# The first transfers and the first gates of a gated linear attention kernel, put in another order

## The chip, the cores and the metric

The kernel runs on one core of one Trainium2 chip. Its engines work side by side, each through its own instructions in program order: PE (TensorE) multiplies matrices, DVE (VectorE) and POOL (GpSimd) work element by element, ACT (ScalarE) computes functions such as Exp and Ln, and SP (SyncE) issues most of the transfers (DMAs) from the main memory. Semaphores make one engine wait for another or for a transfer. The metric is the time of one execution on the device in microseconds; lower is better.

## The reference

The first half is a linear attention with a forget gate, over 4 batches, 8 heads, 768 positions and a head size of 48. The second half is a feed-forward layer with a convolution of three taps along the sequence, of width 1024. Cut to what matters:

```python
def _attn_ref(q, k, v, f_logit):
    f = 1.0 / (1.0 + np.exp(-f_logit))
    for t in range(S):
        state = f[:, :, t, :, None] * state + np.einsum('bhd,bhe->bhde', k[:, :, t], v[:, :, t])
        y[:, :, t] = np.einsum('bhd,bhde->bhe', q[:, :, t], state)

def _moe_ref(x, w_in, conv_w, w_out):
    h = np.maximum(x @ w_in, 0.0)
    conv_out = sum(conv_w[k] * hp[:, k:k + S, :] for k in range(3))   # hp: h with a row of zeros at each end
    gate = 1.0 / (1.0 + np.exp(-conv_out))
    return (h * gate) @ w_out
```

q, k, v and f_logit are float32. The three weights are float64; the kernel reads them as pairs of 32-bit words and makes float32 of them on the chip.

## The kernel before, in words

The sequence of each batch is cut into 6 chunks of 128 positions, so that there are 24 chunks in all, numbered 0 to 23. For each chunk the kernel loads f, k, q and v (256 KB each), takes the logarithm of the gates, sums it along the chunk, scales k and q by the exponentials of these sums and then works with products of matrices: scores inside the chunk, and a state that goes from chunk to chunk. The result of three chunks feeds half a batch of the feed-forward layer. There each product is computed in three parts, a rounded high part and a low part of both factors, so that every weight needs a high and a low version before its first use.

The names of the profile belong to these steps, written as generators that do one instruction, or one group of them, each time they are called:

- `load_f` (line 255, tile `fb`), `load` (line 268, tiles `k` and `q`) and `load_v` (line 273): the transfers of a chunk, all issued by SP.
- `gate` (lines 260 and 263, ACT): Exp, then Ln with 1 added, both in place in `fb`. Up to chunk 8 each chunk has these two of its own.
- `summed` (line 281, PE): the product of `fb` with a triangle of ones gives the sums `pl`, for chunks 0 to 5; later chunks use a scan on DVE.
- `decays` (lines 294 and 296, ACT): the exponentials `fi` and `fd` of these sums, with either sign.
- `scaled_k` and `scaled_q` (lines 305 and 309; DVE for the first chunks): `k` times `fi`, `q` times `fd`.
- `turned` (line 315): transposes of k (`ptk`) on PE, copied to `kp` by ACT.
- `scores` (line 328 on PE into `pa`; line 330 on DVE, copied through a mask into `am`), `values` (line 364 on PE into `py`, first from the state, then from `am` and `v`), `state` (line 339 on PE into `pk`).
- `load_w_in` (line 209, tile `wis`, 512 KB) loads a sixth of the first weight matrix. `single` makes float32 of it: two steps on POOL (lines 173 and 175, into `mswi`), two on ACT (177 and 179), two on DVE (181 and 183). `split` rounds to a high part on ACT (186) and takes the low part on DVE (189). `load_cw` (line 234) brings the weights of the convolution (24 KB, tile `cws`) through the same `single`, its steps named `mscw`.
- `carried` (line 400, ACT): a small copy to the margin of the tile `hb`.
- `warm` (line 522, PE): 12 products of zeros, `pz`, that keep PE at work in the first microseconds; two more stand ahead of them (line 165, `pw`).

No scheduler puts these steps in order. The string `ORDER` (lines 27 to 81) lists them by hand, and a loop at the end calls one step for each word:

```python
for e in ORDER.split():
    next(todo[e], None)
```

`F1` is the load of f for chunk 1, `x1` a step of its gates, `L0` and `M0` the loads of k and q for chunk 0, `V0` that of v, `I0.0` the load of the first piece of the weight, `J0.0` a step of `single` for it, `c` a step of the convolution's weights, `h0.4` the copy to the margin, `w` one product of zeros, `G0` the sum, `p0` an exponential, `K0` and `Q0` the scaling of k and q, `k0` a step of the transpose, `a0` of the scores, `y0` of the values. As each engine keeps to the program's order, this string sets the order of the instructions on each engine and of the transfers in SP's queue. The first words, up to the second chunk's transposes, are:

```
F1 F0 I0.0 L0 c M0 x1 F2 h0.4 L1 x0 I1.0 x0 M1 x1 w G0 V0 J0.0 I2.0 J0.0 w F3 p0 c G1 c L2 p0 K0 M2 J0.0 t0 Q0 J0.0
J0.0 h0.6 w c x2 k0 p1 a0 p1 c c J0.0 J1.0 K1 y0 x2 J1.0 a0 H0.0 w k0 G2 ...
```

So PE has, after the products of zeros and the sums of chunks 0 and 1, the transposes, the scores and the first part of the values of chunk 0, and then the sums of chunk 2 (`G2`), which need the second `x2`. On ACT that second `x2` stands behind `p0`, two steps of `J0.0`, one of `c`, the first `x2` and `p1`.

Of the kernel before, what the change touches and what calls it, by code (L numbers as in the profile page):

```python
# [24 lines left out]
K0 = 24  # L25
K1 = 24
ORDER = """
F1 F0 I0.0 L0 c M0 x1 F2 h0.4 L1 x0 I1.0 x0 M1 x1 w G0 V0 J0.0 I2.0 J0.0 w F3 p0 c G1 c L2 p0 K0 M2 J0.0 t0 Q0 J0.0
J0.0 h0.6 w c x2 k0 p1 a0 p1 c c J0.0 J1.0 K1 y0 x2 J1.0 a0 H0.0 w k0 G2 J1.0 Q1 J1.0 w F7 H0.0 y0 I2.1 c L3 J1.0 J2.0
s0 y0 F4 p2 a1 y0 V1 p2 J2.0 s0 I0.1 K2 x3 t1 w V2 w c Q2 F5 x3 t2 w k2 M3 J2.0 c J1.0 k1 x7 w L4 J2.1 w J2.0 J2.0 w w  # L30
I1.1 x7 G3 a1 V3 k2 h0.0 y1 p3 G7 k1 a2 H1.0 x4 K3 y1 p3 J2.0 x4 t3 H1.0 s1 J2.1 O3 y1 L5 k3 a2 O0 G4 J0.1 J2.1 F6
# [654 lines left out]
```

## Time and profile before

| | before |
|---|---|
| median of 3 runs | 318.06 us (317.87 to 319.04) |
| profiled execution | 319.3 us, of which the span is 317.5 us |
| PE busy | 308.5 us (97%) |
| DVE busy | 254.5 us (80%) |
| ACT busy | 224.9 us (71%) |
| POOL busy | 65.9 us (21%) |
| DMA, mean over the span | 116 GB/s |

The span runs from the first instruction of the profiled execution to the last, and all places in time below count from its start. A busy share is the part of the span in which an engine had an instruction at work. Idle time is given with what ended it: "[1.32 <-DVE k L305]" means that the engine stood still for 1.32 us until DVE was done with tile `k` at line 305. The chain of waits follows the last instruction back, at each step to what released it.

### The profile page before, as it was taken

Reading aid. Unit: us, or ns where it says so; the run is one execution under the profiler, and the core shown is the slowest. Engines: PE = TensorE matmul, PEld = TensorE weight load, DVE = VectorE, ACT = ScalarE, POOL = GpSimd, SP = SyncE. Lnnn points to the kernel's source line nnn. Section 1 sums busy time; section 2 is a strip of 40 time slices with the busy share of each in tenths; the row PEclk is TensorE's granted clock in tenths of the full one; section 3 lists DMA queues with packets and bytes.
Section 4 is the critical chain, followed back from the end, with each engine's and each line's share of the span. In section 5 each row is a group of like instructions: output and inputs, shape, how many; then the busy total and the mean of one; then the engine's idle time right before and its main releaser. Section 6 shows DMA issues by size and latency. Waiting matters only on the chain.

```text
span 317.5 us, 7925 instructions
## 1 busy us (share of the span) xinstructions
PE 308.5 (97%) x3275; PEld 284.1 (89%) x3275; DVE 254.5 (80%) x379; ACT 224.9 (71%) x424; POOL 65.9 (21%) x87
## 2 busy tenths in 40 slices
PE   7699999999999999999999999999999999999995
PEld 4478988989999999999999989998899999999994
DVE  3799999999999999898868779885994596459730
ACT  5789998997898898788842995558453936585531
POOL 2654446244401050050040210054000000000000
PEclk9999999999999999999999999999999999999999
DMA  6989953690303700911074520521002001000021
GB/s 206 355 273 395 359 172 127 244 320 18 97 2 101 250 2 32 308 69 35 16 247 136 176 71 1 151 83 35 2 0 85 0 2 52 25 2 26 25 78 53
DMA packets 19370, 36.74 MB, mean 116 GB/s; under 512 B 2156, under 2 KB 5252, under 8 KB 19332
## 3 DMA queue, kind: packets, MB, share of 16 engines
q1 hardware_dynamic: 19044, 35.82, 33.4%
q8 instruction: 27, 0.44, 0.6%
q10 hardware_dynamic: 288, 0.39, 0.3%
q14 instruction: 11, 0.09, 0.1%
HBM read 31.48 MB, written 4.72 MB: 114 GB/s over the span
## 4 chain that ended last, share of the span: by engine, by line
PE 91%; DVE 3%; DMA 2%; POOL 1%; ACT 1%; issue 0%; SPq 0%; DVEq 0%
PE po L472 32%; PE ph L419 31%; PE py L364 13%; PE pa L328 8%; PE pk L339 4%; PE ptk L315 3%; DMA wis<-in_moe_w_in_dram 2%; PE pl L281 1%; DVE gl L460 1%; PE pz L522 1%; DVE st L349 0%; DVE am L330 0%; POOL mswi L175 0%; SPq L255 0%; POOL mscw L175 0%
## 5 line engine op out<-in xcount | busy, mean ns | idle before, releaser
L419 PE MATMUL ph<-xT,wih 128*128 128x384 f32 x384 | 101.2, 344 | 0.0
L419 PEld LDWEIGHTS ph<-xT,wih 128*128 128x128 f32 x384 | 68.2, 188 | 1.6 <-ACT hb L422 0.2
L472 PE MATMUL po<-woh,gh 128*128 128x384 f32 x192 | 64.8, 338 | 0.0
L472 PE MATMUL po<-wol,gh 128*128 128x384 f32 x192 | 64.7, 337 | 0.0
L472 PE MATMUL po<-woh,gl 128*128 128x384 f32 x192 | 64.6, 336 | 0.0
L419 PE MATMUL ph<-xT,wil 128*128 128x384 f32 x192 | 64.6, 336 | 0.0
L309 POOL TENSOR_TENSOR q<-q,fd 128x512 f32<-128x512 f32 x19 | 27.2, 1438 | 103.4 <-ACT hb L400 43.3
L429 DVE SCALAR_TENSOR_TENSOR g<-hb,cw,g 128x384 f32<-128x384 f32 (+1 forms) x64 | 38.5, 620 | 12.0 <-ACT g L427 11.9
L422 ACT ACTIVATE hb<-ph 128x384 f32<-128x384 f32 x64 | 30.5, 489 | 23.4 <-PE ph L419 22.6
L460 DVE TENSOR_TENSOR gl<-g,gh 128x1024 fp32r<-128x1024 f32 (+4 forms) x34 | 34.9, 1038 | 7.5 <-ACT gh L458 7.4
L431 DVE SCALAR_TENSOR_TENSOR g<-hb,cw,g 128x384 f32<-128x384 f32 (+1 forms) x64 | 39.2, 638 | 0.1
L427 ACT ACTIVATE g<-hb,cw 128x384 f32<-128x384 f32 (+1 forms) x64 | 38.1, 616 | 1.7 <-DVE gl L460 1.4
L440 DVE SCALAR_TENSOR_TENSOR g<-g,hb 128x768 f32<-128x768 f32 (+1 forms) x32 | 30.2, 956 | 11.4 <-ACT g L438 11.4
L458 ACT CAST gh<-g 128x1024 fp32r<-128x1024 f32 (+4 forms) x34 | 26.8, 802 | 15.8 <-PE po L472 15.0
L472 PEld LDWEIGHTS po<-woh,gh 128*128 128x128 f32 x192 | 36.0, 188 | 0.8 <-issue 0.2
L472 PEld LDWEIGHTS po<-wol,gh 128*128 128x128 f32 x192 | 36.1, 188 | 0.0
L419 PEld LDWEIGHTS ph<-xT,wil 128*128 128x128 f32 x192 | 36.1, 188 | 0.0
L472 PEld LDWEIGHTS po<-woh,gl 128*128 128x128 f32 x192 | 36.0, 188 | 0.0
L438 ACT ACTIVATE g<-g 128x768 f32<-128x768 f32 (+1 forms) x32 | 26.5, 848 | 11.0 <-DVE g L431 10.9
L330 DVE COPY_PREDICATED am<-mask,pa 128x1024 f32<-128x1024 uint8 x24 | 31.8, 1327 | 3.0 <-PE pa L328 3.0
L328 PE MATMUL pa<-q,k 48*128 48x128 f32 x384 | 27.9, 285 | 0.4 <-DVE q L309 0.4
L328 PEld LDWEIGHTS pa<-q,k 48*128 48x128 f32 x384 | 23.3, 187 | 4.2 <-issue 2.5
(83 smaller groups left out, 424.2 us busy)
## 6 DMA issues: line engine op xcount, KB each, us to landing
fb<-in_f_logit_dram SPq DMA_DIRECT2D x24, 256.0 KB, 4.4
k<-in_k_dram SPq DMA_DIRECT2D x24, 256.0 KB, 4.8
q<-in_q_dram SPq DMA_DIRECT2D x24, 256.0 KB, 4.4
v<-in_v_dram SPq DMA_DIRECT2D x24, 256.0 KB, 4.8
out_dram<-ob SPq DMA_DIRECT2D x22, 192.0 KB, 2.0
wis<-in_moe_w_in_dram SPq DMA_DIRECT2D x6, 512.0 KB, 6.9
wos<-in_moe_w_out_dram SPq DMA_DIRECT2D x8, 384.0 KB, 5.0
out_dram<-ob ACTq DMA_DIRECT2D x2, 192.0 KB, 1.9
```

Of the source, the lines that this page charges most:

```text
L309: (nc.vector if n < QV else nc.gpsimd).tensor_tensor(raw["q", n], raw["q", n], fds[n][1], ALU.mult)
L328: nc.tensor.matmul(pa[:, j, p, :], kT[r, p, :], qT[r, p, :], start=True, stop=True)
L330: nc.vector.copy_predicated(a_b[n % 2], mask, pa)
L364: nc.tensor.matmul(py[o:o + G, t, :], lhs, rhs, start=len(todo) < 4, stop=len(todo) >= total - 4)
L419: nc.tensor.matmul(ph, w, xts[b, hf][:, t, xl, :], start=(k == 0), stop=(k == 3 * KT - 1))
L422: nc.scalar.activation(hb[:, 2:HS + 2], ph, AF.Relu, scale=0.5)
L427: nc.scalar.activation(cv, hb[:, 1:n + 1], AF.Copy, scale=cw[:, 1, f:f + 1])
L429: nc.vector.scalar_tensor_tensor(cv, hb[:, 2:n + 2], cw[:, 2, f:f + 1], cv, ALU.mult, ALU.add)
L431: nc.vector.scalar_tensor_tensor(cv, hb[:, 0:n], cw[:, 0, f:f + 1], cv, ALU.mult, ALU.add)
L440: nc.vector.scalar_tensor_tensor(cv, cv, 1.0, h_b[:, fp:fp + 2, 1:n + 1], ALU.add, ALU.mult)
L460: nc.vector.tensor_tensor(lo, g[:, f:f + k], hi.bitcast(F32), ALU.subtract)
L472: nc.tensor.matmul(po, g[:, f, :], w, start=(i == 0), stop=(i == 3 * NF - 1))
```

## The change

Only the first words of `ORDER` are different:

```diff
-F1 F0 I0.0 L0 c M0 x1 F2 h0.4 L1 x0 I1.0 x0 M1 x1 w G0 V0 J0.0 I2.0 J0.0 w F3 p0 c G1 c L2 p0 K0 M2 J0.0 t0 Q0 J0.0
+F0 L0 M0 F1 I0.0 c x0 F2 h0.4 L1 x0 I1.0 x1 M1 x1 w G0 V0 J0.0 I2.0 J0.0 w F3 p0 c G1 c L2 p0 K0 M2 J0.0 t0 Q0 J0.0
```

In SP's queue the transfers stood in the order f of chunk 1, f of chunk 0, first piece of the weight, k, the convolution's weights, q. Now they stand f, k, q of chunk 0, f of chunk 1, first piece of the weight, the convolution's weights. From f of chunk 2 on the queue is the same. On ACT the order was Exp of chunk 1, the small copy, Exp and Ln of chunk 0, Ln of chunk 1. Now it is Exp of chunk 0, the small copy, Ln of chunk 0, Exp and Ln of chunk 1. PE, DVE and POOL keep their instructions in the same order. Nothing is added or taken away.

## The prediction

> **What bounds the kernel now.** I began with the head of the profile page, then split the span into stretches in the view of busy time by window (start:end, length, busy microseconds of PE, PEld, DVE, ACT and POOL, granted clock, DMA share, GB/s).
>
> ```profile
> span 317.5 us, 7925 instructions
> PE 308.5 (97%) x3275; PEld 284.1 (89%) x3275; DVE 254.5 (80%) x379; ACT 224.9 (71%) x424; POOL 65.9 (21%) x87
> ```
>
> ```profile
> 8.93:16.00 7.07, 4.36 (x55) 3.19 (x54) 5.70 (x8) 5.04 (x12) 4.77 (x7) 1.00 0.92 341
> 16.00:317.00 301.00, 297.30 (x3199) 276.65 (x3198) 246.04 (x366) 215.13 (x405) 58.86 (x66) 1.00 0.32 107
> 2.13:8.93 6.80, 6.79 (x23) 4.27 (x23) 1.81 (x5) 3.53 (x8) 0.92 (x6) 1.00 0.87 295
> ```
>
> PE executes in program order and the change leaves its instructions alone, so the end moves by what PE's idle time moves. Of that, 2.71 us (7.07 - 4.36) lie between 8.93 and 16 us; before, from 2.13 on, there is none (6.80 against 6.79). After 16 us there are 3.7 us, nearly all behind the last matmul. So the change is decided between 8.93 and 16, and its largest gain is 2.71 us, 0.85% of the span.
>
> What PE waited for there is in the view of waits (total, times, longest); the first line is VectorE's wait, further up the chain.
>
> ```profile
> DVE k L305 <- DMA k<-in_k_dram: 5.3, 1, 5.3
> ...
> PE ptk L315 <- DVE k L305: 1.3, 1, 1.3
> ...
> PE pl L281 <- ACT fb L263: 1.0, 1, 1.0
> ...
> PE pa L328 <- DVE q L309: 0.4, 1, 0.4
> ```
>
> PE's three waits are 2.7 us together: two for the first k and q, and a last one for the logarithm of chunk 2's gates. The last decides: whatever PE does sooner, it stands before `pl` of chunk 2 until that logarithm is done. The chain of waits (start, duration) says where the logarithm's time comes from.
>
> ```profile
> 1.82 6.89 DMA wis<-in_moe_w_in_dram
> ...
> 8.79 0.65 POOL mswi L173
> ...
> 9.51 1.17 POOL mswi L175
> ...
> 10.75 0.62 POOL mscw L173
> ...
> 11.45 0.78 POOL mscw L175
> ...
> 12.46 0.61 ACT fb L260
> ...
> 14.24 0.53 ACT fb L263
> ...
> 14.81 1.16 PE pl L281 x8
> ```
>
> The chain starts with the first weight, not with k or q. It lands at 8.71, GpSimd works on it and on the conv weights, and ScalarE, in order, has the steps that wait for GpSimd ahead of chunk 2's gates. The change delays that weight.
>
> **The change part by part: when things land.** Issues on SP's queue (start, duration), then the landings (size, microseconds from issue), in the order f of chunk 1, f of chunk 0, weight, k, q.
>
> ```profile
> 0.92 0.86 SPq L255 DMA_DIRECT2D fb<-in_f_logit_dram  x2
> 1.82 0.43 SPq L209 DMA_DIRECT2D wis<-in_moe_w_in_dram  x1
> 2.29 0.43 SPq L268 DMA_DIRECT2D k<-in_k_dram  x1
> ...
> 3.26 0.36 SPq L268 DMA_DIRECT2D q<-in_q_dram  x1
> ...
> 8.72 0.33 SPq L273 DMA_DIRECT2D v<-in_v_dram  x1
> ```
>
> ```profile
> fb<-in_f_logit_dram SPq DMA_DIRECT2D x1, 256.0 KB, 2.7
> fb<-in_f_logit_dram SPq DMA_DIRECT2D x1, 256.0 KB, 2.9
> wis<-in_moe_w_in_dram SPq DMA_DIRECT2D x1, 512.0 KB, 6.9
> k<-in_k_dram SPq DMA_DIRECT2D x1, 256.0 KB, 7.1
> q<-in_q_dram SPq DMA_DIRECT2D x1, 256.0 KB, 6.8
> ```
>
> They landed at 0.92 + 2.7 = 3.62, at about 1.35 + 2.9 = 4.25, at 8.71, at 2.29 + 7.1 = 9.39 and at 3.26 + 6.8 = 10.06: in order, one behind the other. A 256 KB transfer behind another takes 10.06 - 9.39 = 0.67 us (the first two: 0.63). The weight, 512 KB, took 8.71 - 4.25 = 4.46, where 2 x 0.67 = 1.34 would be its share by size. No row says why.
>
> In the new order f lands at 3.62, k at 4.29, q at 4.96, f of chunk 1 at 5.63. The weight comes fifth. If its 4.46 us go with it, it lands at 5.63 + 4.46 = 10.09. If the slowness belongs to that stretch of time instead, the same five transfers end when they ended before, at 10.06. Both say 10.1, 1.4 us later, and I take that. The ends: 5.63 + 1.34 = 7.0 if the slowness was an accident of that execution, and about 11.5 if k and q, now early, lose some 0.7 us each as well (half of the weight's excess, 4.46 - 1.34 = 3.1, spread over the two).
>
> Every issue counts: V of chunk 0 was issued at 8.72, just when the weight had landed at 8.71; eight transfers stood between start and wait. In the new order the one eight places ahead is q, so V and the next weight are issued earlier and f of chunk 3 waits for the first weight. These stand in a queue that is busy at 0.92 in this window and will not land sooner; I cost them at nothing.
>
> **What becomes of the gates.** ScalarE's rows (start, duration, idle time before and its cause):
>
> ```profile
> 3.68 0.63 ACT L260 ACTIVATE fb<-fb 128x512 f32<-128x512 f32 x1 [1.52 <-DMA fb<-in_f_logit_dram]
> ...
> 4.97 1.15 ACT L263 ACTIVATE fb<-fb 128x512 f32<-128x512 f32 x2
> 7.60 0.60 ACT L294 ACTIVATE fi<-pl 128x512 f32<-128x512 f32 x1 [1.48 <-PE pl L281]
> ...
> 10.71 0.63 ACT L177 ACTIVATE mswi<-mswi 128x512 f32<-128x512 f32 x1 [2.02 <-POOL mswi L175]
> ...
> 11.81 0.18 ACT L400 COPY hb<-going 128x4 f32<-128x4 f32 x1
> 12.25 0.31 ACT L177 ACTIVATE mscw<-mscw 24x128 f32<-24x128 f32 x1 [0.26 <-POOL mscw L175]
> ```
>
> Chunk 0's logarithm comes some 0.5 us sooner, but PE has no gap before 8.93: `pl` of chunk 0 stands behind the warm-up matmuls, and the `fi` at 7.60 waited for it. No gain. Chunk 1's exponential now waits for a transfer landing at 5.63: 5.7 + 0.63 + 0.58 = 6.9, still ahead of 7.60. Cost nothing, with 0.7 us to spare; beyond that, ScalarE's idle 2.02 us before 10.71 hide it.
>
> **What becomes of k and q.** With `fi` done at 8.20 and k long there, k is scaled from 8.25 instead of 9.50, and q behind it.
>
> ```profile
> 9.50 0.69 DVE L305 TENSOR_TENSOR k<-k,fi 128x512 f32<-128x512 f32 x1 [5.32 <-DMA k<-in_k_dram]
> ...
> 10.15 1.06 DVE L309 TENSOR_TENSOR q<-q,fd 128x512 f32<-128x512 f32 x1
> ```
>
> ```profile
> 26.08 0.62 POOL L175 TENSOR_SCALAR mswi<-mswi 128x512 f32<-128x512 f32 x1
> ```
>
> PE goes on at about 9.0 instead of 10.25, and the waits of 1.3 and 0.4 us nearly disappear. The second effect is on GpSimd: its first L175 took 1.17 us beside VectorE's k and q, and 0.62 at 26.08, where VectorE does neither. In the new order both are done by 8.25 + 0.69 + 1.06 = 10.0 at the latest, before GpSimd starts: 0.55 us back on the chain.
>
> **The sum.** Weight at 10.1; L173 10.18 to 10.83; L175 10.90 to 11.52; ScalarE's L177 at 11.55 (before: 10.71). From L177 to the end of the copy behind L179 there were 11.99 - 10.71 = 1.28 us; the conv weights' L177 then follows at 12.83, without its 0.26 us of waiting, since GpSimd's two conv steps (0.62 and 0.78 beside VectorE) are shorter without k and q. That is 12.83 against 12.25, 0.6 us later (0.85 at most, if those two steps stay as long). Behind it all is in order on ScalarE: `pl` of chunk 2 at 15.4 instead of 14.81. VectorE's chain behind L177 (the mask, then `py`) moves with it. From 16 us on PE has no slack, so it is given back nowhere: 319.3 us of the profiled execution (1.8 above its span) become 319.9. The median of the runs is 1.2 below that execution; by the same 0.19% it goes to **318.7**.
>
> [...] PE's three waits become one. It has 4.36 us of work in the window, 1.2 of them from 14.81 on, so 3.2 to do from 9.0: done at 12.3, then idle to 15.4, 3.1 us, where the longest stop so far was 1.3. What a cold PE costs shows at the start:
>
> ```profile
> 2.14 3.78 PE L165 MATMUL pw<-am 128*128 128x512 f32 x4 [2.14 <-DVE am L134]
> ...
> 7.32 0.48 PE L522 MATMUL pz<-wih 128*128 128x512 f32 x1
> ```
>
> The four matmuls of 512 columns took 0.95 us each, and 0.48 at 7.32: half speed for the first 4 to 5 us. The granted clock reads 1.00 in all windows and doesn't tell it. [...]
>
> **The rivals.** *The weight isn't slow again (0.22).* Its 4.46 us are 3.3 times its share by size, and the rows show it once. Landing at 7.0 to 9.4, GpSimd saves its 0.55 us and the conv wait, and `pl` of chunk 2 comes earlier: at 8.7, as before, by 0.8 us (1.4 less than the sum), so 317.3. At 7.9 it is 1.6 us; the floor is some 2.3 us (PE's work ends at 12.3), 315.8. For it: the 0.67 us steps; against: the reading by the stretch of time gives 10.06 whatever the order. [...]
>
> *The weight comes later still (0.10).* It decides from a landing at 11.1 on: 2.4 - 0.8 = 1.6 us, up to 2 us at 11.5: 319.7 to 320.1, slower.
>
> *PE cools (0.07).* [...]
>
> *The waits for k and q are the bound (0.03).* Then 1.3 + 0.4 us go: 316.4. Against it: the third wait on the list.
>
> *It does nothing (0.03)*, if the transfers run side by side rather than in the order issued: 318.1. Against it: the ordered landings.
>
> **How the numbers follow.** My forecast, a weight landing between 9.6 and 10.8, has 0.55. About 0.5% (1.6 us) is what a measurement of this kernel can tell from no change; the three runs spread over 1.2. Faster by more: 0.06 of the first rival and the 0.03: 0.09. Slower: 0.10 + 0.07 = 0.17. The rest, 0.74, lies within. The range leaves out PE's cooling, the floor of the first rival and the wait for k: 317.0 to 320.1.
>
> **What would show it.** Right: k scaled near 8.3 with no wait on its DMA; first L175 near 0.62 us; the weight landing near 10.1; PE waiting once, some 3 us, before `pl` of chunk 2 near 15.4, on ScalarE's logarithm; no change after 16 but the shift. Wrong: the weight at or before 8.7, `pl` of chunk 2 before 14.5, or matmuls at twice their time behind the stop.

## The result and the profile after

The changed kernel takes 320.50 us (median of 15 runs, 319.04 to 322.92); the kernel before, beside it, 318.58 us (15 runs, 317.28 to 319.59). The ratio is 1.0068 (95% interval 1.0042 to 1.0094): the change makes the kernel slower by 2.2 us by the ratio (the medians differ by 1.9). The forecast of 318.7 us and its range, 317.0 to 320.1, are too low. The profiled execution of the changed kernel took 322.07 us, with a span of 320.3; its mean granted clock was 0.995, that of the kernel before 1.000.

The head of the page and three stretches of time, the first two as before the change and the third from 16 to 33 us, in the view of busy time by window (start:end, length, busy microseconds of PE, PEld, DVE, ACT and POOL, granted clock, DMA share, GB/s):

```profile
span 320.3 us, 7925 instructions
PE 309.9 (97%) x3275; PEld 285.0 (89%) x3275; DVE 252.1 (79%) x379; ACT 225.1 (70%) x424; POOL 63.7 (20%) x87
```

```profile
2.13:8.93 6.80, 5.51 (x15) 3.04 (x15) 1.81 (x5) 2.66 (x7) 0.77 (x5) 1.00 0.89 278
8.93:16.00 7.07, 4.66 (x57) 3.51 (x58) 4.47 (x7) 4.99 (x12) 4.03 (x7) 1.00 0.93 356
16.00:33.00 17.00, 17.00 (x273) 13.76 (x273) 15.83 (x26) 14.53 (x32) 6.25 (x11) 0.90 0.86 297
```

PE is idle for 1.29 us ahead of 8.93, where it had no gap before, and for 2.41 instead of 2.71 us behind. That is 1.0 us more idle time in all, less than half of the loss. The rest is in the third line: PE is busy without a gap from 16 to 33 us, but the granted clock of that stretch is 0.90, where the kernel before has 1.00. The view of PE's waits (total, times, longest) now has one large entry, and the waits for k and q are gone:

```profile
PE pl L281 <- ACT fb L263: 3.7, 2, 2.4
PE pw L165 <- DVE am L134: 2.1, 1, 2.1
PE pa L328 <- POOL q L309: 0.5, 1, 0.5
```

The chain of waits (start, duration):

```profile
2.77 7.14 DMA wis<-in_moe_w_in_dram
...
9.99 1.20 POOL mswi L173
...
11.26 0.63 POOL mswi L175
...
11.91 0.63 ACT mswi L177
...
13.20 0.21 ACT mscw L177
13.41 0.52 ACT fb L260
...
15.09 0.52 ACT fb L263
...
15.66 1.16 PE pl L281 x8
16.82 0.35 PE pz L522
17.17 1.86 PE py L364 x32
19.03 1.05 PE pk L339 x16
...
36.13 5.29 PE ph L419 x30
```

The weight lands at 2.77 + 7.14 = 9.91 instead of 8.71, and chunk 2's sums start at 15.66 instead of 14.81, 0.85 us later. Then something is lost that no wait names: the 32 matmuls of `py` take 1.86 us and the 16 of `pk` 1.05. In the kernel before, the same chain has:

```profile
16.20 1.01 PE py L364 x32
17.21 0.62 PE pk L339 x16
...
33.80 5.30 PE ph L419 x30
```

From the sums of chunk 2 to the first run of 30 matmuls of the hidden layer there are 33.80 - 14.81 = 18.99 us before and 36.13 - 15.66 = 20.47 us after: 1.48 us more for the same instructions with PE never idle. The granted clock by windows of one microsecond in the changed kernel shows why:

```profile
15.00:16.00 1.00, 0.34 (x3) 0.34 (x4) 1.00 (x2) 1.00 (x3) 0.92 (x2) 1.00 0.44 162
16.00:17.00 1.00, 1.00 (x9) 0.73 (x7) 1.00 (x2) 1.00 (x4) 0.08 (x1) 0.89 0.10 35
17.00:18.00 1.00, 1.00 (x21) 0.83 (x24) 1.00 (x3) 0.60 (x2) 0.00 (x0) 0.50 0.41 49
18.00:19.00 1.00, 1.00 (x22) 0.57 (x14) 0.81 (x3) 0.00 (x0) 0.70 (x1) 0.50 0.69 227
19.00:20.00 1.00, 1.00 (x20) 0.89 (x16) 0.39 (x1) 0.90 (x3) 0.92 (x3) 0.50 0.99 375
20.00:21.00 1.00, 1.00 (x18) 0.99 (x16) 1.00 (x3) 1.00 (x3) 0.53 (x3) 0.90 0.75 248
```

The clock was at half for (0.11 + 0.50 + 0.50 + 0.50 + 0.10) / 0.50 = 3.4 us, from about 16.8 to 20.2. It fell a microsecond after PE's 2.41 us stop (13.24 to 15.66) had ended.

So the profiled execution's 2.8 us more of span are 0.85 of delay, 1.48 at half clock, and 0.5 behind 36 us (317.5 - 33.80 = 283.7, 320.3 - 36.13 = 284.2). These last 0.5 are PE's wait for GpSimd's q, in the list above. That wait stands in 7 of the 9 traces below, in that of a kernel no slower than before too, and I don't count it as a part of the change. That is not shown: only one execution of the kernel before was profiled, and how often that kernel has the wait is not on record.

The executions fall into two groups by their mean granted clock. One stretch of 3.4 us at half clock in a span of 318 makes it 0.995. Of the 15 runs of the changed kernel, 7 have a mean clock of 0.995 or less; they average 321.9 us. The other 8, at 0.998 to 1.000, average 319.7. The kernel before averages 318.6. So the mean loss of 2.1 us has two parts: 1.1 us that the executions with the clock up have too, and 2.2 us more in 7 of 15, which is 1.0 on average. The 2.2 us fit the clock: from 0.995 to 0.989, the clocks of the 7 runs make some 2.4 us on average (an estimate: what each lacks to 1, times its span). The 1.1 us I put down to the delay; up to 0.5 of it can be the wait for GpSimd's q.

Three single executions, of 429.94 and 498.81 us (the kernel before) and 1687.07 us (the one with the weight later and its stop filled), stand far above all others of their kernels and are left out of every count and ratio.

### The profile page after: what moved, and what is told of

The parts are those of the page before. It is cut to its first block, busy times and chain, and to the rows that moved or that the text cites. A ratio compares the mean times of both kernels' runs of the same rounds, so it can differ in the third digit from the quotient of the medians.

```text
span 320.3 us, 7925 instructions
## 1 busy us (share of the span) xinstructions
PE 309.9 (97%) x3275; PEld 285.0 (89%) x3275; DVE 252.1 (79%) x379; ACT 225.1 (70%) x424; POOL 63.7 (20%) x87
## 4 chain that ended last, share of the span: by engine, by line
PE 88%; DVE 4%; ACT 3%; DMA 2%; POOL 1%; issue 1%; SPq 1%; DVEq 0%
PE po L472 32%; PE ph L419 29%; PE py L364 12%; PE pa L328 7%; PE pk L339 3%; PE ptk L315 3%; DMA wis<-in_moe_w_in_dram 2%; PE pl L281 1%; DVE gl L460 1%; DVE am L330 1%; PE pz L522 1%; POOL q L309 1%; DVE st L349 1%; ACT ob L477 0%; POOL mswi L173 0%
## 5 line engine op out<-in xcount | busy, mean ns | idle before, releaser
L309 POOL TENSOR_TENSOR q<-q,fd 128x512 f32<-128x512 f32 x19 | 28.0, 1476 | 104.4 <-ACT fd L296 39.0
L440 DVE SCALAR_TENSOR_TENSOR g<-g,hb 128x768 f32<-128x768 f32 (+1 forms) x32 | 31.3, 990 | 11.4 <-ACT g L438 11.4
L460 DVE TENSOR_TENSOR gl<-g,gh 128x1024 fp32r<-128x1024 f32 (+4 forms) x34 | 32.7, 973 | 7.5 <-ACT gh L458 7.4
```

The costliest lines, as they stand in the source:

```text
L309: (nc.vector if n < QV else nc.gpsimd).tensor_tensor(raw["q", n], raw["q", n], fds[n][1], ALU.mult)
L440: nc.vector.scalar_tensor_tensor(cv, cv, 1.0, h_b[:, fp:fp + 2, 1:n + 1], ALU.add, ALU.mult)
L460: nc.vector.tensor_tensor(lo, g[:, f:f + k], hi.bitcast(F32), ALU.subtract)
```

## The experiments

Two theories stood against each other. **Cooling**: the change gathers PE's three short stops into a long one, after which the clock falls in about half of the executions; beside that it only delays the first weight by some 1 us. **Delay alone**: the late weight, or the late f of chunk 1, costs everything, and the half clock comes with it or by chance. In the table "cold" counts the executions with a mean granted clock of 0.995 or less, among those whose clock was recorded. The times (us) and PE's longest stop in the window from 8 to 20 us are from the profiled execution of each kernel; "to the 30 `ph`" is the time from the start of chunk 2's sums to the first run of 30 matmuls of the hidden layer.

| kernel | weight lands | chunk 2's sums | to the 30 `ph` | longest stop | cold | ratio to before (95%) |
|---|---|---|---|---|---|---|
| before | 8.71 | 14.81 | 18.99 | 1.3 | 5 of 65 | 1 |
| changed | 9.91 | 15.66 | 20.47 | 2.4 | 7 of 15 | 1.0068 (1.0042 to 1.0094) |
| stop filled | 9.15 | 14.82 | 19.00 | 1.2 | 0 of 12 | 1.0039 (1.0019 to 1.0058) |
| k, q first | 9.54 | 14.94 | 20.75 | 2.4 | 9 of 10 | 1.0068 (1.0041 to 1.0095) |
| gates only | 7.85 | 13.93 | 19.00 | 1.0 | 1 of 12 | 0.9989 (0.9959 to 1.0019) |
| weight later | 9.94 | 15.14 | 20.44 | 2.6 | 5 of 5 | 1.0137 (1.0113 to 1.0161) |
| weight later, filled | 10.32 | 15.53 | 18.99 | 1.1 | 0 of 5 | 1.0085 (1.0062 to 1.0108) |
| short stops longer | 8.06 | 13.49 | 18.99 | 1.6 | 4 of 12 | 1.0030 (1.0002 to 1.0058) |
| chunk 2's gates first | 10.07 | 11.26 | 25.29 | 2.2 | 9 of 12 | 1.0079 (1.0052 to 1.0107) |
| and its k | 9.55 | 12.16 | 22.49 | 1.8 | 4 of 6 | 1.0071 (1.0051 to 1.0091) |
| conv steps later | 8.27 | 13.65 | 20.08 | 0.7 | 3 of 12 | 1.0033 (1.0014 to 1.0053) |

**The stop filled.** The changed kernel, with PE at work in its stop:

```diff
-                nc.tensor.matmul(pz, wz[:, :P], wz, start=True, stop=True)
+            for _ in range(6 if i == 3 else 1):
+                nc.tensor.matmul(pz, wz[:, :P], wz, start=True, stop=True)
```

> The changed kernel with five more products of zeros (0.48 us each, 2.4 us together) on PE in its one stop before the sums of chunk 2; nothing else differs. Cooling theory: the changed kernel loses its time in two parts, about 0.9 us because chunk 2's sums start at 15.66 instead of 14.81, and 1.5 to 3 us in those executions in which PE's clock then falls to half. With the stop filled the clock stays at 1.00 in nearly all executions, and the time is 0.5 to 1.2 us above the kernel before, ratio 1.002 to 1.004. Rival, delay alone: the late weight and waits further on cost all of the 2.2 us and the half clock is only seen beside them; then nothing is gained and the ratio stays at 1.007 or grows.

PE's waits and the chain, as far as they matter:

```profile
PE pl L281 <- ACT fb L263: 2.4, 2, 1.2
```

```profile
2.76 6.39 DMA wis<-in_moe_w_in_dram
...
14.82 1.16 PE pl L281 x8
...
33.82 5.30 PE ph L419 x30
```

Five useless matmuls more, and the kernel is faster: 319.97 us, ratio 1.0039. None of 12 executions was cold, and from chunk 2's sums to the hidden layer it takes the 19.00 us of the kernel before. Cooling predicted this, delay alone did not. What is left over the kernel before should be the delay, but this pair of traces doesn't show it: here the weight landed at 9.15, the sums start at 14.82 against 14.81, and the 0.5 us by which the span is longer are the wait for GpSimd's q. The pair with the weight later, below, shows that a delay costs time of its own.

**One part alone: k and q ahead of the weight.**

```diff
-F1 F0 I0.0 L0 c M0 x1 F2 h0.4 L1 x0 I1.0 x0 M1 x1
+F1 F0 L0 M0 I0.0 c x1 F2 h0.4 L1 x0 I1.0 x0 M1 x1
```

> The kernel before with one part of the change: k and q ahead of the first weight (f of chunk 1, f of chunk 0, k, q, weight), and the gates in the old order. Cooling theory: the weight lands at 9.9 as in the changed kernel; k and q of chunk 0 are scaled from 8.3, so GpSimd isn't held up and chunk 2's sums start near 15.3; PE stops once, for about 3 us, and its clock falls in at least half of the executions: ratio 1.004 to 1.010. Rival, the late gates: what costs is that f of chunk 1 landed at 7.5 and held up ScalarE; f is early here, so the time is that of the kernel before within 0.2%.

```profile
2.77 6.77 DMA wis<-in_moe_w_in_dram
...
14.94 2.08 PE pl L281 x8
...
35.69 5.29 PE ph L419 x30
```

Ratio 1.0068, that of the whole change, and 9 of 10 executions cold. The late f of chunk 1 isn't needed for the loss: it is early here. The sums of chunk 2, which start at 14.94, hardly later than the 14.81 of before, take 2.08 us instead of 1.16, since in this execution the clock had fallen before the stop was over: it is 0.82 from 14 to 15 us and 0.50 from 15 to 18, so it fell at about 14.6, some 2.1 us into a stop of 2.41.

**The other part alone: the order of f and of the gates.**

```diff
-F1 F0 I0.0 L0 c M0 x1 F2 h0.4 L1 x0 I1.0 x0 M1 x1
+F0 F1 I0.0 L0 c M0 x0 F2 h0.4 L1 x0 I1.0 x1 M1 x1
```

> The kernel before with the other part of the change: f of chunk 0 ahead of f of chunk 1 and chunk 0's gates first, while the weight keeps its third place. Cooling theory: weight at 8.7, chunk 2's sums at 14.8, PE's stops spread as before, clock 1.00: ratio 0.998 to 1.002. Rival, the gates' order itself costs or gains: it moves by over 0.3%.

Ratio 0.9989, with 1 in its interval: this part does nothing, as both the prediction and the trace of before (PE without a gap ahead of 8.93) said. In this execution the weight, third in the queue as before, landed at 7.85.

**The weight later still, and the same with the stop filled.** The first edit to the changed kernel, and the second with `9 if i == 3` in place of the 6 shown above:

```diff
-F0 L0 M0 F1 I0.0 c x0 F2 h0.4 L1 x0 I1.0 x1 M1 x1
+F0 L0 M0 F1 c x0 F2 h0.4 L1 x0 I0.0 I1.0 x1 M1 x1
```

> The changed kernel with the first weight two places further back, behind f and k of the next chunks (two transfers of 256 KB, 0.67 us each). Delay and cooling both: the weight lands 1.3 us later than in the changed kernel, chunk 2's sums start 1.3 us later, PE's stop grows to about 3.7 us and its clock falls in nearly every execution: 323 to 324 us, ratio 1.013 to 1.018. Rival, the weight's landing isn't what the sums wait for: as the changed kernel, ratio 1.005 to 1.008. Beside it: between 4 and 8 us only transfers of 256 KB are under way here; if the slowness of that stretch comes with the weight, they land 0.67 us apart.

> The same with eight more products of zeros (3.8 us) in PE's stop before the sums of chunk 2. If delay and half clock are two separate costs, the clock stays up in nearly all executions and the delay alone is left: 1.3 us above the changed kernel with its stop filled, ratio 1.007 to 1.010, and 1.7 us or more below the unfilled one. Rival, filling only helps by chance: no difference to the unfilled one.

Unfilled and filled:

```profile
4.12 5.82 DMA wis<-in_moe_w_in_dram
...
15.14 2.08 PE pl L281 x8
...
35.58 5.30 PE ph L419 x30
```

```profile
4.12 6.20 DMA wis<-in_moe_w_in_dram
...
15.53 1.16 PE pl L281 x8
...
34.52 5.30 PE ph L419 x30
```

The pair shows the half clock by itself: in the filled kernel chunk 2's sums start 0.39 us later, and the hidden layer starts 1.06 us sooner. All 5 executions of the one are cold, none of the other, and the ratios are 1.0137 and 1.0085. Against the changed kernel's pair (1.0068 and 1.0039) each is slower by 0.5 to 0.7%, so the delay is a cost of its own. It is smaller than expected: the weight landed at 9.94 and 10.32, where 11.2 was forecast, the stop was 2.6 us instead of 3.7, and the medians (322.53 and 321.04 us) are 1.5 us apart where at least 1.7 was said. Of the transfers ahead of it q took 1.5 us and the others 0.6 to 0.8, so the slowness of that stretch is not the weight's alone.

**The short stops made longer.** The kernel before, with three of its products of zeros cut to 8 columns:

```diff
-            nc.tensor.matmul(pz, wz[:, :P], wz, start=True, stop=True)
+            m = 8 if i in (1, 2, 3) else WC
+            nc.tensor.matmul(pz[:, :m], wz[:, :P], wz[:, :m], start=True, stop=True)
```

> The kernel before with three of its products of zeros (those between the sums of chunks 0 and 2) cut from 512 to 8 columns: PE is idle some 1.4 us more between 8 and 16 us, but in three separate stops, none over 2 us, and nothing that anyone waits for is later. If one long stop is what lowers the clock, it falls in at most 3 of 12 executions and the ratio is 0.998 to 1.003. Rival, the sum of the idle time lowers it: it falls in over half of them, ratio 1.004 to 1.009.

Four of 12 executions were cold, and the ratio is 1.0030 (1.0002 to 1.0058): between the two expectations. This settles little. In the profiled execution, whose clock stayed up, the weight landed at 8.06 and chunk 2's sums start at 13.49; PE's longest stop is 1.6 us instead of 1.3, but from 2.13 to 16 us PE is idle for 2.0 us, less than the 2.7 of before. No cold execution was profiled, and of the kernel before 1 of 16 executions beside these was cold. That idle time in short stops brings the clock down is therefore not shown here.

**Chunk 2's gates ahead of the weight's steps.** This and the next two were to find a version that beats both kernels. From the kernel before: both f, k, q and f of chunk 2 are issued ahead of the weight, and the order of steps becomes

```diff
-F1 F0 I0.0 L0 c M0 x1 F2 h0.4 L1 x0 I1.0 x0 M1 x1 w G0 V0 J0.0 I2.0 J0.0 w F3 p0 c G1 c L2 p0 K0 M2 J0.0 t0 Q0 J0.0
-J0.0 h0.6 w c x2 k0 p1 a0 p1 c c J0.0 J1.0 K1 y0 x2 J1.0 a0 H0.0 w k0 G2 J1.0 Q1 J1.0 w F7 H0.0 y0 I2.1 c L3 J1.0 J2.0
+F0 F1 L0 M0 F2 I0.0 c x0 h0.4 L1 x0 I1.0 x1 M1 x1 w G0 V0 I2.0 w F3 p0 G1 L2 p0 K0 M2 t0 Q0 J0.0 J0.0 c c
+x2 x2 w k0 p1 a0 p1 y0 a0 w K1 k0 G2 Q1 J0.0 J0.0 J0.0 h0.6 c c c J0.0 J1.0 J1.0 H0.0 J1.0 J1.0 w F7 H0.0 y0 I2.1 c L3 J1.0 J2.0
```

> Both f first, then k, q and f of chunk 2, then the weight; and in the order of steps chunk 2's gates, chunk 1's exponentials and chunk 0's mask stand ahead of ScalarE's and VectorE's steps on the first weight. If chunk 2's sums wait only because the weight's steps stand ahead of them, they now start between 11 and 13, PE has no stop over 1.5 us, the clock stays at 1.00 and the time falls below the kernel before by 0.5 to 2.2 us (ratio 0.993 to 0.9985). Rival: the weight's later steps, or v of chunk 0, become the wait in their place and PE stands still there; then it is within 0.2% of the kernel before or slower.

Chunk 2's sums start at 11.26, as intended, and the kernel is slower, ratio 1.0079. The view of PE's waits from 14 us on has the new stop:

```profile
PE ptk L315 <- DVE k L305: 2.2, 1, 2.2
```

PE now runs out of work at 17.7 and stands until 19.92 before the transposes of chunk 2. They wait for k of chunk 2, whose exponential stands on ScalarE behind the second weight's steps. The clock fell at 19.1 and stayed down for 6.8 us in this execution. The stop was not removed but moved. The fall came 1.4 us after PE had run out of work, and in the 3.4 us ahead of it (as long as the changed kernel's clock was at half) PE was idle for only 1.5 us. So here the clock fell before PE had stood for 2 us at a stretch.

**And chunk 2's k too.** From the kernel just shown:

```diff
-x2 x2 w k0 p1 a0 p1 y0 a0 w K1 k0 G2 Q1 J0.0 J0.0 J0.0 h0.6 c c c J0.0 J1.0 J1.0 H0.0 J1.0 J1.0 w F7 H0.0 y0 I2.1 c L3 J1.0 J2.0
-s0 y0 F4 p2 a1 y0 V1 p2 J2.0 s0 I0.1 K2 x3 t1 w V2 w c Q2 F5 x3 t2 w k2 M3
+x2 x2 w k0 p1 a0 p1 y0 a0 w K1 k0 G2 J0.0 J0.0 J0.0 Q1 p2 p2 h0.6 c c c J0.0 K2 J1.0 J1.0 H0.0 J1.0 J1.0 w F7 H0.0 y0 Q2 I2.1 c L3 J1.0 J2.0
+s0 y0 F4 a1 y0 V1 J2.0 s0 I0.1 x3 t1 w V2 w c F5 x3 t2 w k2 M3
```

> As the kernel with chunk 2's gates first, and chunk 2's exponentials and its k too ahead of the second weight's steps. If that kernel only lost because PE then stood 2.2 us before the transposes of chunk 2, PE now has no stop over 1.5 us, the clock stays up, and the time is 0.5 to 1.5 us below the kernel before (ratio 0.995 to 0.9985). Rival: VectorE and ScalarE have no time to spare before the first hidden layer, so the weights come later in their place and PE waits there: the ratio is 0.999 or more.

Ratio 1.0071. The stop moved again, to the transpose of the conv weights (`PE pc L240 <- DVE c L183: 1.8, 1, 1.8`), and the hidden layer starts at 34.65 instead of 33.80. Four of the 6 executions are cold, and yet they take no longer than the other two (320.6 against 320.7 us on average). PE is idle for 3.0 us between 16 and 33 us in this execution, and I suppose, without having shown it, that the half clock is hidden in such waits.

**The conv weights' steps behind chunk 2's gates.** The gates-only kernel, with three words `c` moved behind `a0`:

```diff
-J0.0 h0.6 w c x2 k0 p1 a0 p1 c c J0.0 J1.0 K1 y0 x2 J1.0 a0 H0.0 w k0 G2
+J0.0 h0.6 w x2 k0 p1 a0 p1 J0.0 J1.0 K1 y0 x2 J1.0 a0 c c c H0.0 w k0 G2
```

> The kernel before with chunk 0's gates first (which alone changed nothing) and ScalarE's and VectorE's three steps on the conv weights behind chunk 2's gates instead of ahead of them. If the chain from the weight's landing to chunk 2's sums sets the start, its length falls from 6.1 us to about 5.4 (0.26 us of waiting and two steps of 0.21 us leave it), the end moves by as much, and the ratio is 0.996 to 1.000, with the clock up. Rival: VectorE's later steps become the wait and nothing is gained, or PE's stops grow and its clock falls more often: ratio 1.000 or more.

From the landing to chunk 2's sums it is 13.65 - 8.27 = 5.38 us, as expected, instead of 6.1. But from there to the hidden layer it is 20.08 us instead of 18.99, in an execution whose clock stayed up: several waits of 0.2 to 0.3 us for VectorE's masks and states take it back. Ratio 1.0033, with 3 of 12 executions cold, though no stop of the profiled one is longer than 0.7 us. No version here beats the kernel before.

## Why the prediction was wrong, point by point

**The mechanism of the delay was right, and so was its start.** The weight was to land at 10.1 and landed at 9.91; that it came so close is partly luck, since the same queue landed it at 9.15 in the filled kernel. PE's waits for k and q went, and a stop before chunk 2's sums took their place, which started at 15.66 where 15.4 was said. That stop was 2.41 us long and not 3.1, because PE had lost 1.28 us before chunk 1's sums, which the prediction did not foresee, and ran out of work at 13.24 instead of 12.3. Behind the sums PE has no slack: it takes 18.99 or 19.00 us to the hidden layer in every kernel that leaves the steps behind these sums alone and whose clock stayed up in the profiled execution.

**The step that failed is the rival "PE cools".** Its chance was 0.07, and the range left it out. No run shows the term behind so low a chance, a limit above the 3.1 us of the forecast; the runs showed the clock down at shorter stops. A stop of 2.4 us was enough in 7 of 15 executions of the changed kernel, and one of 2.4 to 2.6 us in 14 of 15 of two others (k, q first; weight later), with each stop read from the one profiled execution; where chunk 2's gates come first, the fall came 1.4 us into the stop. The sign that the prediction named for it, matmuls at twice their time behind the stop, is what the trace shows (`py` at 1.86 us instead of 1.01). Half speed for 4 to 5 us, as at the kernel's start, would lose 2 to 2.5 us (an estimate from the rows of that start), and cold executions of the changed kernel are 2.2 us longer than its others. The longest stop between matmuls in the trace of before, with the clock at 1.00 behind it, was 1.3 us; between that and the 3.1 us of the forecast nothing had been measured. The changed kernel's stretch at half clock lasted 3.4 us. In the 3.4 us ahead of its fall at about 16.8 PE had 2.3 us of idle time and more than 1 us of work. In the kernel with chunk 2's gates first 1.5 us of idle time in the 3.4 us ahead of the fall were enough, while the kernel before kept its clock with 1.7 us (1.32 and 0.36) in the 3.4 us from 8.93 on. So 1.5 us of idle time in 3.4 were enough in one profiled execution, and 1.7 us in 3.4 were not in another; how much is needed, these runs do not tell.

**The delay was under-priced, 0.6 us where 1.1 were measured.** Two steps of it failed. First, of chunk 1's exponential, which was to wait for f "landing at 5.63": "Cost nothing, with 0.7 us to spare". The rows of landings (size, microseconds from issue) and of ScalarE say otherwise:

```profile
q<-in_q_dram SPq DMA_DIRECT2D x1, 256.0 KB, 3.9
fb<-in_f_logit_dram SPq DMA_DIRECT2D x1, 256.0 KB, 5.3
```

```profile
7.57 0.63 ACT L260 ACTIVATE fb<-fb 128x512 f32<-128x512 f32 x1 [2.60 <-DMA fb<-in_f_logit_dram]
...
8.76 0.58 ACT L294 ACTIVATE fi<-pl 128x512 f32<-128x512 f32 x1
```

q landed at 1.82 + 3.9 = 5.7 and f of chunk 1 at 2.29 + 5.3 = 7.6. The slowness that the kernel before showed at the weight struck the transfers that now stood in that stretch of time. Of my two readings of the 4.46 us, the one by time was the better; both gave the same landing for the weight, but not for what stood ahead of it. So ScalarE waited 2.60 us, PE stood for 1.28 us before chunk 1's sums, `fi` came at 8.76 instead of 7.60, and k was scaled at 9.38, hardly sooner than the 9.50 of before.

Second, "0.55 us back on the chain" for GpSimd. k and q were now scaled just when the weight landed:

```profile
9.38 0.69 DVE L305 TENSOR_TENSOR k<-k,fi 128x512 f32<-128x512 f32 x1 [5.20 <-ACT fi L294]
9.99 0.69 DVE L309 TENSOR_TENSOR q<-q,fd 128x512 f32<-128x512 f32 x1
```

```profile
9.99 1.19 POOL L173 TENSOR_SCALAR mswi<-wis 128x512 f32<-128x512 f32 x1 [7.08 <-DMA wis<-in_moe_w_in_dram]
11.26 0.62 POOL L175 TENSOR_SCALAR mswi<-mswi 128x512 f32<-128x512 f32 x1
```

GpSimd's L175 fell to 0.62 us as said, but its L173, 0.65 before, took 1.19 beside q: the longer time moved one step ahead. From the landing to chunk 2's sums there are 5.75 us, against 5.3 in the sum and 6.10 before. Where k and q were out of the way in time ("weight later"), it is 5.20. L173 takes 0.65 us where q's L309 is not beside it (the kernel before, gates only), and 0.85, 1.11 and 1.19 where the two overlap for 0.33, 0.61 and 0.69 us (k and q first, stop filled, changed). In the rows above, 1.19 is 0.65 and most of q's 0.69.

A third part is the base. The kernel before was priced from one execution in which the weight landed at 8.71. In three other kernels that have it third in the queue it landed at 7.85, 8.06 and 8.27, so an earlier base would make the delay larger than the 0.85 us between the two traces. How much of the 1.1 us each of these parts holds, and how much the wait for GpSimd's q, is not shown.

**What was right** beside these: the order of the gates brought nothing (ratio 0.9989 alone); the issues that change places in SP's queue cost nothing that a wait shows; PE had no slack behind 16 us to give a delay back.

**What stays open** is why the transfers between 4 and 8 us are slow, what exactly the clock weighs, why a few executions of kernels without a long stop (5 of 65 of the kernel before, 4 of 12 and 3 of 12 of two others) are cold as well, and whether the change makes the wait of 0.5 us for GpSimd's q more frequent.

## What to carry to other kernels

Where one engine bounds the kernel and works in program order, the last of its waits sets the end: inputs that come sooner for the steps ahead of that wait only gather the idle time in front of it (here the waits of 1.3 and 0.4 us for k and q went, and the last one grew from 1.0 to 2.4). On TensorE one long stop was worse here than three short ones of about the same sum: the mean granted clock was 0.995 or less in 9 of 10 executions with one stop of 2.4 us, and in 5 of 65 with three stops of 2.7 us together. So look at the granted clock of every execution, not only at the idle time, and if the stop can't be removed, fill it (0 of 17 executions cold here). Before a transfer is moved back, ask which chain begins at it: here the first weight, which looked like the least urgent of the first five, stood at the head of the chain that set the start.

## What the runs showed of the hardware that was not expected

In the four kernels whose profiled execution has a stop of 2.2 to 2.6 us, the mean granted clock was 0.995 or less in 30 of 42 executions. In three of those profiled executions the fall to 0.50 can be placed: 1.1 us behind the stop (changed), 2.1 us into it (k and q first) and 1.4 us into it (chunk 2's gates first). The clock stayed there for 3.4 us in the first two and 6.8 in the third. With the stop filled by useless matmuls the mean clock was 0.997 to 1.000 in 17 of 17 executions. And a transfer of 256 KB, which in the kernel before landed 0.67 us behind another (q behind k), took up to 1.9 us between 4 and 8 us: q 1.5 and f of chunk 1 1.9 in the changed kernel, q 1.5 and the three behind it 0.6 to 0.8 with the weight later still.
